# Threshold attention and a SwiGLU block on one core: another order for the first loads, and weight steps that begin one segment later

## The chip, the core and the metric

The kernel runs on one core of one Trainium2 chip. The metric is the device time of one execution in microseconds. The median of three runs of the kernel before is 1515.48 us (1515.47 to 1515.57).

## The reference

Attention over 8 batches of 8 heads, 576 positions, head width 64, with a threshold on the scores, then a gated block of width 512 to 1536 to 512 on the 4608 rows that come out:

```python
scores = scale * np.matmul(q, k.transpose(0, 1, 3, 2))
thresh = np.max(scores, axis=-1, keepdims=True) - tau
scores = np.where(scores >= thresh, scores, -1000000000.0)
scores = scores - np.max(scores, axis=-1, keepdims=True)
attn = np.exp(scores)
attn = attn / (np.sum(attn, axis=-1, keepdims=True) + 1e-09)
x = np.matmul(attn, v)          # heads side by side: (4608, 512)
g = x @ w_gate
out = (g / (1 + np.exp(-g)) * (x @ w_val)) @ w_out
```

Queries, keys and values arrive as 32-bit floats, the three weight matrices as 64-bit floats.

## The kernel before

**Work units.** Two heads of one batch make a pair; a batch has four pairs, and there are 32. A tile is 128 query rows of a pair (64 at the end of it). The main loop goes over segments, each with one pair and a list of its tiles. The first eight segments belong to batch 0: segments 0 to 3 take the first two tiles of pairs 0, 1, 2, 3; segments 4 to 7 take the remaining three tiles of pairs 3, 0, 1, 2. All later segments hold a whole pair. In this text the tiles are numbered as they come: T0 to T7 are the eight tiles of segments 0 to 3, and T8, T9, T10 those of segment 4.

**One tile.** `scores` multiplies queries by keys on PE (line 342 in part one; lines 342 and 347 in segments 4 to 7), DVE takes the maximum (L369), ACT makes the threshold (L375) and the exponential (L376), DVE drops what is under the threshold and sums (L380), then adds up and inverts the sums (L404, L405). In tiles T0 to T7 the inverse is put in a diagonal (L416) and enters with the transposition on PE (L448, L451); from T8 on, the rows are scaled before it, one head by ACT (L388) and the other by POOL (L386), and PE transposes them (L446). ACT copies the transposed rows out of PSUM (L454, L459), and one tile later PE multiplies by the values (`attend_tile`, L474 and L478) and ACT copies the product (L480). Scores have two PSUM tiles, so the next tile's L342 waits for L380 of the tile before.

**Preparing a pair.** Keys and queries come into SBUF in rows and are turned in 32x32 blocks on DVE. Queries are scaled first, by POOL (L254). `prepare` turns the keys (L815) and the first 256 query columns (L818); the remaining 320 columns of each query go on a list, `later`, and are turned when there is place for them, in `prepare` (L823) or in segment 4 (L893). The raw keys and queries of pairs 1 and 2 lie in a free buffer, `extra`; all other pairs share one pair of tiles of the pool `ld`, so that a new pair may be loaded only when the old one has been turned.

**Weights.** A weight piece is 768 KB of 64-bit floats. `fetch_weights` loads it (L185, two transfers of 384 KB) into one of a few places, and stops when none is free. `split_weights` makes a high word (L196) and a low word (L197) of it on ACT; there are two buffers for low words. `join_weights` puts them together, with three operations on DVE (L203, L207, L210) and one on POOL (L212), and sets the place free. A tile has at most one such step; `need(n)` makes more on the spot when the block's next product needs `n` pieces and fewer are joined. T10 has a double step.

**The order of the work.** Every engine takes its instructions in the order in which the program writes them. SP issues the loads. From segment 4 on, `fill` puts products of the second block (L536, `pg` and `pv`) between the parts of each tile; `pace` sets how many. `gates` multiplies the gate on POOL (L568). ACT's Exp table is loaded once at the start (L263).

Of the kernel before, what the change touches and what calls it, by code (L numbers as in the profile page):

```python
# [13 lines left out]
AF = mybir.ActivationFunctionType  # L14
ALU = mybir.AluOpType
# [4 lines left out]
def kernel(  # L20
# [30 lines left out]
    nc = tc.nc  # L51
    P = 128
    B, H, S, D = q.shape
    NP = H // 2
# [3 lines left out]
    G = 32  # L58
    NG = P // G
    NJ = S // G  # L60
# [7 lines left out]
    XB = 5  # L68
# [5 lines left out]
    QA = TA * P  # L74
    SCALE = 1.0 / float(D) ** 0.5
# [16 lines left out]
    tau_s = const.tile([P, 1], F32, name="tau_s")  # L92
    cut = const.tile([P, 1], F32, name="cut")
    cap = const.tile([P, 1], F32, name="cap")
    scl = const.tile([P, 1], F32, name="scl")
# [4 lines left out]
    minus2 = const.tile([P, 1], F32, name="minus2")  # L100
    nc.vector.memset(minus2, -2.0)
    junk = const.tile([P, 1], F32, name="junk")
# [6 lines left out]
    free = NP * (S - TA * P)  # L109
# [20 lines left out]
    XW, HW = NCC * TC, NF2 * P  # L130
    xall = const.tile([P, XB * XW + 2 * HW], F32, name="xall")
# [4 lines left out]
    extra = const.tile([P, 3 * NF2 * DM2], F32, name="extra")  # L136
# [36 lines left out]
    def fetch_weights(n=1):  # L173
        for _ in range(n):
            if not wpieces or wpieces[0][2] in used:
                return
            dst, srcs, place = wpieces.popleft()
            used.add(place)
            m = 2 if len(srcs) == 2 else nf
            to = places[place].bitcast(U64).rearrange("p (m n) -> p m n", m=m)  # L180
            if len(srcs) == 1:
                nc.sync.dma_start(out=to, in_=srcs[0])
            else:
                for x, src in enumerate(srcs):
                    nc.sync.dma_start(out=to[:, x, :], in_=src)  # L185
            fetched.append((dst, place))
# [44 lines left out]
    def load_qk(i):  # L231
        b, hp_ = divmod(i, NP)
        tiles = {}

        free = {1: 0, 2: 1}.get(i)
        srcs = {"q": (q, "(j r) (e d) -> e r j d"),
                "k": (k, "(j r) (e d) -> e r j d" if b == 0 else "(r j) (e d) -> e r j d")}
        for x, name in enumerate("qk"):
            if free is None:
                tiles[name] = ld.tile([P, NJ, G], F32, name=f"{name}raw")  # L240
            else:
                n = 2 * free + x
                tiles[name] = extra[:, n * S:(n + 1) * S].rearrange("p (j d) -> p j d", d=G)
        raws = [tiles[name].rearrange("p j d -> p (j d)") for name in "qk"]

        def load(name, js, queues):
            src, order = srcs[name]
            for g in range(NG):
                h, e = divmod(g, 2)
                queues[g // 2].dma_start(out=tiles[name][g * G:(g + 1) * G, js],  # L250
                                         in_=src[b, 2 * hp_ + h].rearrange(order, r=G, d=G)[e][:, js])

        def scale(cs):
            nc.gpsimd.tensor_scalar(out=raws[0][:, cs], in0=raws[0][:, cs], scalar1=scl, scalar2=None, op0=ALU.mult)  # L254

        if i == 0:

            both = [nc.sync, nc.scalar]
            load("k", slice(0, NJ), both)
            nc.scalar.dma_start(out=tau_s, in_=tau.partition_broadcast(P))  # L260
            load("q", slice(0, QA // G), both)

            nc.scalar.activation(junk, minus2, AF.Exp)  # L263
            nc.vector.tensor_scalar(out=scl, in0=tau_s, scalar1=0.0, scalar2=SCALE, op0=ALU.is_ge, op1=ALU.mult)
            nc.vector.tensor_scalar(out=cap, in0=tau_s, scalar1=0.0, scalar2=2e38, op0=ALU.is_ge, op1=ALU.mult)
            nc.vector.tensor_scalar(out=cap, in0=cap, scalar1=-1e38, scalar2=None, op0=ALU.add)
            nc.vector.scalar_tensor_tensor(out=cut, in0=tau_s, scalar=-1.0, in1=cap, op0=ALU.mult, op1=ALU.min)

            def load_rest():
                load("q", slice(QA // G, NJ), [nc.sync] * 2)  # L270
                scale(slice(QA, S))

            more_loads.append(load_rest)
        else:
            for name in "kq" if i == 1 else "qk":
                load(name, slice(0, NJ), [nc.sync] * 2)
            scale(slice(0, S))
            while more_loads:
                more_loads.pop()()
        return raws  # L280

    def load_v(seg):
# [481 lines left out]
    segs = [{"i": i, "tiles": early, "halved": False} for i in range(NP)]  # L764
# [27 lines left out]
        return rate  # L792

    raws = {}
    more_loads = []
    kept = {}
    later = []

    def fetch_qk(i):
        if i < NPAIR and i not in raws and i not in kept:  # L800
            raws[i] = load_qk(i)

    def prepare(seg):

        i = seg["i"]
        if i in kept:
            seg.update(kept[i])
            return
        qr, kr = raws[i]
        kept[i] = None  # L810
        qT = qkp.tile([P, S], F32, name="qT")
        if i < NP:
            kT = pall[:, 4 + i, :]
            rest = flat[:, i * (S - QA):(i + 1) * (S - QA)]
            nc.vector.transpose(out=kT, in_=kr)  # L815
            if i == 0:
                nc.vector.tensor_scalar(out=qr[:, 0:QA], in0=qr[:, 0:QA], scalar1=scl, scalar2=None, op0=ALU.mult)
            nc.vector.transpose(out=qT[:, 0:QA], in_=qr[:, 0:QA])  # L818

            later.append((rest, qr[:, QA:S]))  # L820
            if i >= NP - 2:
                to, fr = later.pop(0 if i == NP - 2 else -1)
                nc.vector.transpose(out=to, in_=fr)  # L823
            kept[i] = {"kT": kT, "qT": rest, "q0": QA}
        else:
            kT = qkp.tile([P, S], F32, name="kT")
            nc.vector.transpose(out=kT, in_=kr)
            nc.vector.transpose(out=qT, in_=qr)
        seg.update(kT=kT, qT=qT, q0=0)

    def give(n):
        for u in segs[n]["gives"]:
            ready.append(u)
            left[0] += cost(u)
        gains[n] = (gains[n][0], 0)
# [2 lines left out]
    fetch_qk(0)  # L838
    prepare(segs[0])
    fetch_qk(1)  # L840
    fetch_weights(2)
    load_v(segs[0])
    fetch_weights(2)
    prev, last = None, iter(())
    for n, seg in enumerate(segs):
        if NP <= n < 2 * NP:
            seg["v"] = segs[seg["i"]]["v"]
        for x, t in enumerate(seg["tiles"]):
            go = scores(seg, t)
            next(go)  # L850
            if not n and not x:
                run_idle(6)
            next(last, None)
            attends = prev is not None and x == 1
            products = iter(())
            attend_tile()
            next(go)
            next(last, None)
            flip()
            if n == NP and x == 0:  # L860
                attend_tile()
                give(n - 1)
            if n == 2 * NP and x == 1:
                give(n - 1)
            if attends and n > 2 * NP:
                if prev["i"] % NP == 0:
                    need(NW)
                    start_batch(prev["i"] // NP)
                products = attend(prev)
            part = pace(n, x) / 2  # L870
            more = len(split)
            if n or x:
                split_weights()
                fetch_weights(2)
            if x == 0 and n >= NP:
                fetch_qk(seg["i"] + 1)
            next(go)
            double = t == NT and NP <= n < NP + 2
            if more and not double:
                join_weights()  # L880
            fill(part)
            next(go)
            fill(part)
            if double:

                join_weights(2)
                split_weights()
                fetch_weights(2)
            gates()
            last = go  # L890
            if n == NP and later:
                to, fr = later.pop(0)
                nc.vector.transpose(out=to, in_=fr)  # L893
            if attends and n > 2 * NP:
                next(products)
                next(products)
                give(n - 1)
            if attends and seg["halved"]:
                load_v(seg)
            if x == 0 and 0 < n < NP:  # L900
                load_v(seg)
            if x == len(seg["tiles"]) - 2 and n + 1 < len(segs):
                prepare(segs[n + 1])
                if n < NP:
                    fetch_qk(segs[n + 1]["i"] + 1)
        prev = seg
    next(last)
    next(last)
# [40 lines left out]
```

## Time and profile before

| | us | share |
|---|---|---|
| span | 1513.8 | |
| PE busy | 1486.9 | 98% |
| DVE busy | 995.8 | 66% |
| ACT busy | 726.2 | 48% |
| POOL busy | 641.2 | 42% |
| first weight product (L536) begins | 66.97 | |

The shares are means over the span. In the first 67 us PE only does attention, and its work waits on chains through DVE and ACT; later the weight products fill it. The tables that the prediction shows come from three views: busy time by stretches (with the granted PE clock, 1.00 being full speed), instructions in order of time (start, length, engine, line, operands, and in brackets the idle time before it and what ended it), and the issues of transfers in the same list, under the names SPq and ACTq.

### The profile page before, as it was taken

To read this page: it belongs to the slowest core of one execution; us is meant where nothing else is said; L and a number is where in the kernel's file an instruction comes from. 1 tells how busy PE (TensorE), PEld (TensorE's weight loads), DVE (VectorE), ACT (ScalarE), POOL (GpSimd) and SP (SyncE) were. 2 spreads that over 40 slices of the span, in tenths; PEclk is the share of its full clock that TensorE was granted. 3 is DMA by queue.
4 is the path that set the end of the run, shared out by engine and by line. 5 is a ranking of instruction groups with operands and counts; after the bars stand their busy time and mean duration, and the time that the engine had idled before them with its cause. 6 is when DMAs were issued, how large, how long until landed. Compare 5 with 4: busy or idle time off the path is not lost. (4 is left out here: it accounts for less than half of the span.)

```text
span 1513.8 us, 31488 instructions
## 1 busy us (share of the span) xinstructions
PE 1486.9 (98%) x11808; PEld 1126.7 (74%) x11808; DVE 995.8 (66%) x3040; ACT 726.2 (48%) x2158; POOL 641.2 (42%) x637
## 2 busy tenths in 40 slices
PE   8999899999999999999999999999999999999999
PEld 6777664477777777787777777777777777888887
DVE  6878988777777777747767666776676767512212
ACT  5877665555455555434545444454544454311110
POOL 2355544367453545336444444553545353500000
PEclk9999999999999999999999999999999999999999
DMA  8542411211112111112111111211110220000000
GB/s 184 156 140 92 100 37 39 54 33 32 47 32 47 31 23 35 40 31 41 38 21 33 25 47 33 46 33 47 33 33 15 47 48 16 1 14 1 15 15 15
DMA packets 176872, 66.93 MB, mean 44 GB/s; under 512 B 159696, under 2 KB 159696, under 8 KB 176720
## 3 DMA queue, kind: packets, MB, share of 16 engines
q1 hardware_dynamic: 172416, 56.83, 16.5%
q0 software_dynamic: 2432, 7.87, 1.4%
q8 instruction: 94, 1.54, 0.4%
q14 instruction: 58, 0.48, 0.1%
q10 hardware_dynamic: 1872, 0.21, 0.1%
HBM read 55.44 MB, written 9.44 MB: 43 GB/s over the span
## 5 line engine op out<-in xcount | busy, mean ns | idle before, releaser
L386 POOL TENSOR_SCALAR pall<-pall,ri 128x288 f32<-128x288 f32 (+1 forms) x260 | 265.2, 1030 | 344.7 <-DVE ri L396 314.2
L536 PE MATMUL pv<-xall,wgv 128*128 128x256 f32 x1728 | 405.6, 383 | 3.0 <-ACT pall L454 2.7
L536 PE MATMUL pg<-xall,wgv 128*128 128x256 f32 x1728 | 403.2, 382 | 0.2 <-ACT pall L454 0.2
L536 PEld LDWEIGHTS pv<-xall,wgv 128*128 128x128 f32 x1728 | 324.7, 191 | 68.8 <-issue 21.9
L536 PEld LDWEIGHTS pg<-xall,wgv 128*128 128x128 f32 x1728 | 323.6, 190 | 65.5 <-issue 22.0
L357 DVE TENSOR_REDUCE mx<-sc 128x2 f32<-128x576 f32 x252 | 180.5, 750 | 237.4 <-PE sc L334 236.6
L380 DVE SCALAR_TENSOR_TENSOR pall<-sc,th,pall 128x288 f32<-128x288 f32 (+1 forms) x540 | 258.0, 527 | 33.2 <-ACT pall L376 33.2
L376 ACT ACTIVATE pall<-sc,nm 128x288 f32<-128x288 f32 (+1 forms) x540 | 236.3, 510 | 0.6
L372 ACT ACTIVATE th<-nm,cut 128x4 f32<-128x4 f32 (+1 forms) x140 | 41.6, 297 | 383.7 <-DVE nm L361 383.7
L568 POOL TENSOR_TENSOR ht<-ht,gt 128x512 f32<-128x512 f32 x84 | 107.0, 1274 | 194.1 <-DVE ht L556 105.8
L425 DVE STREAM_TRANSPOSE pall<-pall 128x576 f32<-128x576 f32 x252 | 181.3, 754 | 2.8 <-POOL pall L386 2.8
L634 PE MATMUL po<-wo,ht 128*128 128x256 f32 x768 | 177.5, 381 | 0.0
L334 PE MATMUL sc<-kT,qT 64*32 64x288 f32 x4032 | 157.9, 410 | 11.2 <-DVE pall L380 9.9
L634 PEld LDWEIGHTS po<-wo,ht 128*128 128x128 f32 x768 | 144.6, 190 | 26.4 <-issue 6.0
L556 DVE SCALAR_TENSOR_TENSOR ht<-tn,pv 128x512 f32<-128x512 f32 x102 | 69.9, 685 | 132.0 <-PE pv L536 118.7
L388 ACT ACTIVATE pall<-pall,ri 128x288 f32<-128x288 f32 (+1 forms) x264 | 132.9, 553 | 0.0
L310 ACT COPY sums<-sums 32x4 f32<-32x4 f32 (+1 forms) x560 | 108.4, 194 | 49.9 <-DVE pall L380 38.6
L549 ACT ACTIVATE tn<-pg 128x512 f32<-128x512 f32 x108 | 64.8, 600 | 139.8 <-PE pg L536 133.0
L500 PE MATMUL xa<-pall,vall 64*64 64x288 f32 x2016 | 128.7, 405 | 0.0
L334 PEld LDWEIGHTS sc<-kT,qT 64*32 64x32 f32 x4032 | 58.7, 105 | 88.8 <-issue 60.0
L500 PEld LDWEIGHTS xa<-pall,vall 64*64 64x64 f32 x2016 | 74.4, 133 | 50.7 <-ACT sums L310 3.6
L652 POOL TENSOR_TENSOR ht<-ht,xall 128x256 f32<-128x256 f32 x48 | 34.1, 727 | 156.3 <-PE po L634 155.1
(106 smaller groups left out, 1339.5 us busy)
## 6 DMA issues: line engine op xcount, KB each, us to landing
vall<-in_v_dram SPq DMA_DIRECT2D x112, 144.0 KB, 3.5
kraw<-in_k_dram SPq DMA_DIRECT2D x118, 72.0 KB, 2.9
qraw<-in_q_dram SPq DMA_DIRECT2D x116, 72.0 KB, 2.5
out_dram<-ob POOLq DMA_DIRECT2D x28, 256.0 KB, 2.9
wo<-in_moe_w_gate_dram SPq DMA_DIRECT2D x16, 384.0 KB, 3.7
wo<-in_moe_w_val_dram SPq DMA_DIRECT2D x16, 384.0 KB, 4.3
xall<-in_moe_w_out_dram SPq DMA_DIRECT2D x5, 768.0 KB, 4.9
wo<-in_moe_w_out_dram SPq DMA_DIRECT2D x3, 768.0 KB, 4.6
```

The source lines that it names most:

```text
L310: nc.scalar.copy(out, in_[:, :, 0])
L334: nc.tensor.matmul(ps[g * G:(g + 1) * G, h, 0:SH], qT[hs, col + a * G:col + (a + 1) * G], kT[hs, c * SH:(c + 1) * SH], start=True, stop=True)
L357: nc.vector.tensor_reduce(out=mx[:, 2 * x:2 * x + 2, 0], in_=tile_[:, :, 0:SH], axis=AX.X, op=ALU.max, negate=True)
L376: nc.scalar.activation(ps[x], scs[x], AF.Exp, bias=nm[:, x:x + 1])
L380: nc.vector.scalar_tensor_tensor(out=ps[x], in0=scs[x], scalar=th[:, x:x + 1], in1=ps[x], op0=ALU.is_ge, op1=ALU.mult, accum_out=sm[:, x, ...
L386: nc.gpsimd.tensor_scalar(out=ps[x], in0=ps[x], scalar1=ri[:, x:x + 1], scalar2=None, op0=ALU.mult)
L388: nc.scalar.activation(ps[x], ps[x], AF.Copy, scale=ri[:, x:x + 1])
L425: nc.vector.transpose(out=p, in_=p)
L500: nc.tensor.matmul(xa[a][h * D:(h + 1) * D, at:at + n * G].rearrange("d (i q) -> d i q", q=G), vr[rs, h, j, :], p[rs, lo:lo + n, j, :], st ...
L536: nc.tensor.matmul(ps[:, i], wgv[:, mat, c, (f + i) * P:(f + i + 1) * P], x[:, c, cs], start=(c == 0), stop=(c == NCC - 1))
L568: eng.tensor_tensor(out=hts[x], in0=hts[x], in1=gt, op=ALU.mult)
L634: nc.tensor.matmul(ps, h(f), w[:, f, :], start=(f == 0), stop=(f == NF2 - 1))
```

## The change

At the start, the change loads only what the first eight tiles use: keys and the first 256 query columns, of all four pairs. Pairs 0 and 1 use the queues of SP and ACT, the values of pair 0 follow, then pair 2, two weight pieces, pair 3, and two more pieces. The remaining query columns come in segments 1 to 3, pair 3's first. Pair 3 gets a place of its own in `xall`, so that only pair 0 lies in the shared tiles of `ld` in batch 0. Three remaining parts, instead of two, are turned in segment 4. Pair 4 is loaded in segment 4 instead of segment 3. Weight steps begin with the third tile instead of the second. Its aim is that the first pairs aren't held up by weights and by query columns that are used only later.

```diff
-        free = {1: 0, 2: 1}.get(i)
+        places_ = {1: extra[:, 0:2 * S], 2: extra[:, 2 * S:4 * S], 3: xall[:, XB * XW:XB * XW + 2 * S]}
...
-        if i == 0:
-            both = [nc.sync, nc.scalar]
-            load("k", slice(0, NJ), both)
-            nc.scalar.dma_start(out=tau_s, in_=tau.partition_broadcast(P))
-            load("q", slice(0, QA // G), both)
-            nc.scalar.activation(junk, minus2, AF.Exp)
...
+        if i < NP:
+            queues = [nc.sync, nc.scalar if i < 2 else nc.sync]
+            load("k", slice(0, NJ), queues)
+            if i == 0:
+                nc.scalar.dma_start(out=tau_s, in_=tau.partition_broadcast(P))
+            load("q", slice(0, QA // G), queues)
...
+            else:
+                scale(slice(0, QA))
             def load_rest():
                 load("q", slice(QA // G, NJ), [nc.sync] * 2)
                 scale(slice(QA, S))
             more_loads.append(load_rest)
         else:
-            for name in "kq" if i == 1 else "qk":
+            for name in "qk":
                 load(name, slice(0, NJ), [nc.sync] * 2)
             scale(slice(0, S))
-            while more_loads:
-                more_loads.pop()()
...
-            if i >= NP - 2:
-                to, fr = later.pop(0 if i == NP - 2 else -1)
+            if i == NP - 1:
+                to, fr = later.pop()
                 nc.vector.transpose(out=to, in_=fr)
...
     fetch_qk(1)
+    nc.scalar.activation(junk, minus2, AF.Exp)
+    load_v(segs[0])
+    fetch_qk(2)
     fetch_weights(2)
-    load_v(segs[0])
+    fetch_qk(3)
     fetch_weights(2)
...
-            if n or x:
+            if 0 < n < NP and x == 0:
+                if n == 1:
+                    more_loads.rotate(1)
+                    more_loads.popleft()()
+                more_loads.popleft()()
+            if n:
                 split_weights()
                 fetch_weights(2)
...
                 prepare(segs[n + 1])
-                if n < NP:
-                    fetch_qk(segs[n + 1]["i"] + 1)
```

More of the change, by code (lines that the diff above doesn't have):

```diff
@@ L238, in load_qk @@
         for x, name in enumerate("qk"):
-            if free is None:
+            if i in places_:
+                tiles[name] = places_[i][:, x * S:(x + 1) * S].rearrange("p (j d) -> p j d", d=G)
+            else:
                 tiles[name] = ld.tile([P, NJ, G], F32, name=f"{name}raw")
-            else:
-                n = 2 * free + x
-                tiles[name] = extra[:, n * S:(n + 1) * S].rearrange("p (j d) -> p j d", d=G)
         raws = [tiles[name].rearrange("p j d -> p (j d)") for name in "qk"]
@@ L254, in scale @@
             nc.gpsimd.tensor_scalar(out=raws[0][:, cs], in0=raws[0][:, cs], scalar1=scl, scalar2=None, op0=ALU.mult)
-        if i == 0:
-            both = [nc.sync, nc.scalar]
-            load("k", slice(0, NJ), both)
-            nc.scalar.dma_start(out=tau_s, in_=tau.partition_broadcast(P))
-            load("q", slice(0, QA // G), both)
-            nc.scalar.activation(junk, minus2, AF.Exp)
[L264 to L267, printed above, removed]
+        if i < NP:
[4 more added lines that the diff above has]
+            load("q", slice(0, QA // G), queues)
+            if i == 0:
+                nc.vector.tensor_scalar(out=scl, in0=tau_s, scalar1=0.0, scalar2=SCALE, op0=ALU.is_ge, op1=ALU.mult)
+                nc.vector.tensor_scalar(out=cap, in0=tau_s, scalar1=0.0, scalar2=2e38, op0=ALU.is_ge, op1=ALU.mult)
+                nc.vector.tensor_scalar(out=cap, in0=cap, scalar1=-1e38, scalar2=None, op0=ALU.add)
+                nc.vector.scalar_tensor_tensor(out=cut, in0=tau_s, scalar=-1.0, in1=cap, op0=ALU.mult, op1=ALU.min)
+            else:
+                scale(slice(0, QA))
             def load_rest():
@@ L794 @@
     raws = {}
-    more_loads = []
+    more_loads = deque()
     kept = {}
```

## The prediction

> **What bounds the kernel now.** I read the page first (busy shares), then a table of stretches, then the engines' instructions in order of time for the first 100 us, then the DMA issues. The page says PE is busy for 98% of the span; the table of stretches says where it isn't (columns: PE, PEld, DVE, ACT, POOL busy, granted PE clock, DMA share, GB/s):
>
> ```profile
> 20.00:28.00 8.00, 8.00 (x68) 6.28 (x67) 4.02 (x10) 5.55 (x13) 2.07 (x2) 1.00 0.89 182
> 28.00:32.00 4.00, 0.27 (x2) 0.03 (x2) 3.67 (x8) 1.91 (x5) 1.42 (x1) 1.00 0.48 90
> ...
> 34.00:38.00 4.00, 4.00 (x26) 2.58 (x24) 2.85 (x4) 1.55 (x5) 3.50 (x2) 0.50 0.94 253
> ...
> 168.00:172.00 4.00, 1.24 (x33) 0.43 (x32) 3.93 (x14) 3.23 (x10) 2.33 (x3) 1.00 0.28 108
> 172.00:176.00 4.00, 4.00 (x24) 3.04 (x11) 3.82 (x12) 1.34 (x5) 2.38 (x2) 0.57 0.02 4
> ...
> 300.00:1500.00 1200.00, 1199.51 (x9530) 935.60 (x9523) 751.27 (x2382) 525.19 (x1652) 507.70 (x535) 1.00 0.14 30
> ```
>
> From 300 us on PE never rests. The change edits only the first 100 us and leaves PE's own instructions and their order as they are. So what PE loses or saves before 300 us goes into the end one for one. Two idle stretches cost twice, because after each the granted clock is 0.50.
>
> The first hole is a late load of pair 2's keys:
>
> ```profile
> 27.92 0.78 DVE L815 STREAM_TRANSPOSE pall<-extra 128x576 f32<-128x576 f32 x1 [2.86 <-DMA extra<-in_k_dram]
> ...
> 32.02 3.07 PE L342 MATMUL sc<-pall,qT 64*128 64x288 f32 x8 [3.75 <-DVE pall L380]
> ...
> 35.02 1.97 PE L474 MATMUL xa<-pall,vall 128*64 128x128 f32 x16
> ```
>
> I number the tiles T0 to T7 (part one) and T8, T9, T10 (the next segment). The time of a tile's first threshold multiply (L380) is my marker: T2 20.99, T3 31.05, T4 38.81, T5 45.93, T6 52.08, T7 57.82 us. In steady state one tile takes 5.74 us (52.08 to 57.82); T3 took 10.06 and T4 7.76.
>
> The second place to see is T8, at 66 to 75 us, where PE meets POOL's scaled probabilities:
>
> ```profile
> 65.75 1.87 POOL L386 TENSOR_SCALAR pall<-pall,ri 128x576 f32<-128x576 f32 x1 [1.91 <-DVE ri L405]
> ...
> 67.96 0.50 DVE L893 STREAM_TRANSPOSE pall<-extra 128x320 f32<-128x320 f32 x1
> ...
> 70.19 1.36 PE L342 MATMUL sc<-pall 64*128 64x288 f32 x10
> ...
> 71.48 1.09 PE L446 MATMUL tp<-pall 128*128 128x128 f32 x8
> ...
> 74.51 2.86 PE L536 MATMUL pv<-xall,wgv 128*128 128x256 f32 x12 [1.40 <-ACT pall L454]
> ```
>
> POOL's L386 ends at 67.62, long before PE's transposes (L446) want it at 72.0.
>
> **What the Trainium skill says.** "TensorE: Matmul & The Clock Gate", Part 1, gives two clock states, and half speed after an idle window of about 3.4 us. The trace agrees and is stricter: the 3.75 us hole was followed by half clock from 32.2 to 39.0 us, and the hole of 2.60 us at 168 by 3.4 us of it. "DMA: Bandwidth & Descriptors", Issuing engines are not separate DMA queues, says that a second issuing queue saves issue time only. I use this for the keys that move to ACT's queue; the trace shows about 0.5 us per issue (4 in 2.12 us at 6.11).
>
> **Part by part.**
>
> *Loads (keys and first queries at once, weights behind).* Pair 2's keys and first queries now stand before all weights: 24 transfers come before the last key transfer, none of them weights, against 40 with eight weight transfers. At 0.53 us per issue on SP, and with the two waits at 3 to 5 us that are there today, the keys are issued by about 11 us and the queries by 13.5; 2.5 us later they have landed. T2's transposes then follow its multiplies at 23.0 without the wait of 2.86 us, and without the weight join that stood before them (0.54+0.56+0.96 = 2.06 us on DVE). T3: transposes end at 24.1, maxima 24.1, exponentials 25.8, L380 at 26.6 instead of 31.05. That is -4.4 us. T0 to T2 stay: their chain runs over PE and ACT (xa L474, then its copy L480 at 19.86, then L375 at 20.02), and the ACT weight step removed in T1 (1.97 us) lay beside PE's work.
>
> *Values of pair 1.* T4 needs them. Now 53 transfers stand before them instead of 41; the 12 more are pair 3's keys, first and remaining queries, which the change issues first. Before, they were issued so:
>
> ```profile
> 25.89 0.50 SPq L296 DMA_DIRECT2D vall<-in_v_dram  x1
> ...
> 27.63 0.51 SPq L297 DMA_DIRECT2D vall<-in_v_dram  x1
> ```
>
> and landed 2.8 us later, at 30.4. In the built program each transfer waits for the one eight before it (the query at 17.74 is issued just when the value load of 12.24 has landed, 5.5 us after). I stepped the new order through with this rule, 0.5 us per issue, 0.54 us of DMA time per 72 KB of keys, 1.15 us per weight transfer, rates fitted to the transfers of before: pair 1's values land at 33.5 us, with 32 to 36 as ends. Without the wait T4's product (L474) would start at 29.7. PE so idles 3.8 us, the clock falls again, and T4's L474 with its tail L478 takes 2.6 us, as before (35.02 to 37.6). From there L480, L375 and L376 take 1.2 us: T4's L380 at 37.3 instead of 38.81. Net -1.5 us of the -4.4; ends -3 (32 us) and +1 (36 us). I take -1.3, a little off for a slower clock in T5. After that DVE sets T5 (join 2.06 and three transposes 1.4) in both kernels.
>
> *Pair 4's queries on POOL: the added wait.* Pair 0's remaining queries keep their place in the load buffer until T8, where L893 turns them. Before, they were turned at 28.95 (L823). Pair 4's queries use the same buffer, were loaded at 44.36, and are now loaded in T8. In the built program their transfers wait for exactly that L893, and POOL's scaling of them (L254) stands in POOL's queue *before* T8's L386. So L386, and behind it the weight joins' last adds (L212), wait for L893, four transfers and a scaling. The trace has this very chain once:
>
> ```profile
> 43.83 0.47 DVE L823 STREAM_TRANSPOSE pall<-qraw 128x320 f32<-128x320 f32 x1
> ...
> 44.36 1.95 SPq L250 DMA_DIRECT2D qraw<-in_q_dram  x4
> ...
> 48.88 1.73 POOL L254 TENSOR_SCALAR qraw<-qraw,scl 128x576 f32<-128x576 f32 x1 [4.03 <-DMA qraw<-in_q_dram]
> ```
>
> 4.58 us from L823's end (44.30) to the scaling, then 1.73. On T8's clock of before: L893 ends at 68.0 (L207 takes 0.56 instead of 0.98 beside an idle POOL), scaling 72.6 to 74.3, L386 to 76.2. PE has done the first head's transposes at 72.0 and waits 4.2 us; behind it stand the second head's four, then pg, then pv. pv starts at 77.4 instead of 74.51: +2.9 us, since it had idled 1.40 before. Ends +2 and +3.5.
>
> *Clock after that.* A hole of 4.2 us leaves some window mostly idle; 3.4 us at half clock cost up to 1.7 us of PE work, 6.8 us up to 3.4. I take +1.7, ends 0.8 and 3.4.
>
> *Weight steps from the third tile on.* One join less in part one: seven pieces are joined by T10 instead of eight, and the gate of the third and fourth blocks needs eight. The missing one comes as an extra step there: DVE 2.06, POOL 1.81, and ACT's split (L197) has only two buffers for its low words and waits for these adds, as it already does for 2.82 us at 88.15. Copy L480 stands behind that split and goes from 89.1 to 90.7; pv at 89.37 waits for its buffer: +1.6 us, ends 0.5 and 2.5. The matmul that needs the eighth piece comes only at 88.7, when the add (86.6) is done.
>
> *Nothing:* the third L893 (0.5 us, DVE idles 2.4 us at T11); splitting the scalings (POOL idles then); the Exp table load behind four more issues on ACT (done near 8, needed at 9.51).
>
> Sum: -1.3 + 2.9 + 1.7 + 1.6 = +4.9, so 1515.5 + 4.9 = 1520.4 us.
>
> **Rivals.**
> *A, they cancel:* values land near 30, no hole in T4. Then T4's L380 is at 32.2, -6.6 us, against +6.2: 1515.1. For it: key and query bytes ahead of the values grow by only 256 KB. Against: eight more issues on SP alone are 4 us.
> *B, faster:* as A, and PE bridges POOL's delay with work in hand: -6.6 + 1.6 = 1510.5. Against: PE takes its queue in order, and pg and pv stand behind the transposes.
> *C, clearly slower:* values land at 36 (+1), both clock losses at their upper end (3.4), queue +3.5, step +2.5: 1525.9.
>
> **How the numbers follow.** Forecast case 0.60, A 0.20, B 0.12, C 0.08. The bound of 0.2% is 3.0 us. Nearly all of the forecast case and C lie above it: slower 0.67; A and the forecast's low end: same 0.19; B and a little of A: faster 0.14. The range from 1512 to 1525 reaches past A on the low side and leaves out B and C, 2 in 10 together.
>
> **What would show it.** Right: no DMA wait before L815 in T2; a PE hole before T4's L474; POOL's L386 in T8 beginning some 9 us after its reciprocal instead of at once, with L254 ahead of it; a PE hole of about 4 us between the halves of T8's L446; 0.50 in the clock column after each. Wrong: T4's L474 at full clock near 30 us (A or B), or L446 in T8 without a hole (B).

## The result, and the profile after

The changed kernel takes 1523.6 us (median of 6 runs, 1523.1 to 1524.7), the kernel before 1515.4 in the same runs. The ratio is 1.0056, with a 95% interval of 1.0043 to 1.0069: 8 us slower, well clear of the noise. From here on line numbers are those of the changed kernel: behind `load_qk` most are one lower (L379 was L380, L385 was L386, L445 was L446, L479 was L480, L535 was L536), in it L249 was L250 and L253 was L254, and the turning of remaining queries in segment 4, L893, is now L902.

First the table of stretches of the changed kernel (columns as in the prediction):

```profile
28.00:32.00 4.00, 1.50 (x10) 0.88 (x8) 3.77 (x9) 3.01 (x6) 0.00 (x0) 1.00 0.85 162
34.00:38.00 4.00, 3.67 (x23) 2.63 (x24) 0.00 (x0) 0.52 (x3) 2.36 (x3) 0.50 0.61 108
72.00:80.00 8.00, 4.36 (x13) 3.73 (x14) 6.44 (x11) 4.99 (x10) 8.00 (x4) 0.66 0.54 133
92.00:96.00 4.00, 1.90 (x12) 1.25 (x10) 4.00 (x8) 1.76 (x2) 1.75 (x1) 1.00 0.58 171
...
300.00:1500.00 1200.00, 1198.71 (x9563) 931.40 (x9564) 755.24 (x2402) 530.40 (x1668) 509.12 (x535) 1.00 0.14 30
```

From 300 us on PE is full, as before. In 72 to 80 us PE now works 4.36 of 8 us at a clock of 0.66 while POOL works all 8, where the kernel before had

```profile
72.00:80.00 8.00, 6.61 (x51) 4.63 (x50) 6.42 (x13) 6.29 (x13) 3.69 (x2) 1.00 0.14 30
```

The stretch from 92 to 96 has a hole of its own. The first hole (28 to 32) is still there, with PE busy for 1.50 us instead of 0.27, but another transfer is late now, as the next lines show.

**Part one.** Instructions of the changed kernel in order of time, and below them the issues of two of the four transfers that bring pair 1's values:

```profile
23.00 0.78 DVE L814 STREAM_TRANSPOSE pall<-extra 128x576 f32<-128x576 f32 x1
...
26.50 0.82 DVE L379 SCALAR_TENSOR_TENSOR pall<-sc,th,pall 128x576 f32<-128x576 f32 x1 [1.09 <-ACT pall L375]
...
33.85 0.66 PE L473 MATMUL xa<-pall,vall 128*64 128x128 f32 x2 [4.36 <-DMA vall<-in_v_dram]
34.85 1.94 PE L473 MATMUL xa<-pall,vall 128*64 128x128 f32 x14 [0.34 <-DMA vall<-in_v_dram]
...
31.30 0.41 SPq L295 DMA_DIRECT2D vall<-in_v_dram  x1
...
32.95 0.51 SPq L296 DMA_DIRECT2D vall<-in_v_dram  x1
```

Pair 2's keys are turned at 23.00 without the wait of 2.86 us, and T3 is 4.5 us earlier (26.50 instead of 31.05). T4's product then waits 4.36 us for pair 1's values, whose transfers are issued 5.4 us later than before (31.30 instead of 25.89).

**T8.** The queue of POOL, and what PE does behind it:

```profile
64.80 0.17 DVE L404 RECIPROCAL ri<-tot 128x2 f32<-128x2 f32 x1
...
66.92 0.50 DVE L902 STREAM_TRANSPOSE pall<-qraw 128x320 f32<-128x320 f32 x1
...
67.46 1.95 SPq L249 DMA_DIRECT2D qraw<-in_q_dram  x4
...
71.86 1.72 POOL L253 TENSOR_SCALAR qraw<-qraw,scl 128x576 f32<-128x576 f32 x1 [8.63 <-DMA qraw<-in_q_dram]
73.56 2.03 POOL L385 TENSOR_SCALAR pall<-pall,ri 128x576 f32<-128x576 f32 x1
...
75.64 1.12 PE L445 MATMUL tp<-pall 128*128 128x128 f32 x4 [4.12 <-POOL pall L385]
...
77.62 4.59 PE L535 MATMUL pv<-xall,wgv 128*128 128x256 f32 x12
```

L385's input has been ready since 65 us (L404 ends at 64.97), but it stands behind L253, which waits for pair 4's queries, and these are issued at 67.46, just when L902 has ended. The twelve `pv` matmuls took 2.86 us before and take 4.59 at the lower clock.

**T10.** In this stretch the kernel before had

```profile
82.76 1.02 DVE L203 TENSOR_SCALAR wgv<-wgv 128x768 f32<-128x768 f32 x2
...
85.73 4.16 POOL L212 TENSOR_TENSOR wgv<-wgv,extra 128x768 uint32<-128x768 uint32 x2 [6.05 <-DVE wgv L210]
...
88.15 1.01 ACT L197 ACTIVATE extra<-wo,minus 128x768 f32<-128x768 uint32 x1 [2.82 <-POOL wgv L212]
...
89.37 1.99 PE L536 MATMUL pv<-xall,wgv 128*128 128x256 f32 x8 [0.31 <-ACT xall L480]
```

and the changed kernel has

```profile
89.67 2.64 DVE L203 TENSOR_SCALAR wgv<-wgv 128x768 f32<-128x768 f32 x2
...
89.89 1.99 POOL L212 TENSOR_TENSOR wgv<-wgv,extra 128x768 uint32<-128x768 uint32 x1 [8.05 <-DVE wgv L210]
94.25 4.16 POOL L212 TENSOR_TENSOR wgv<-wgv,extra 128x768 uint32<-128x768 uint32 x2 [2.37 <-DVE wgv L210]
...
96.67 0.99 ACT L197 ACTIVATE extra<-wo,minus 128x768 f32<-128x768 uint32 x1 [2.91 <-POOL wgv L212]
97.57 0.24 ACT L479 COPY xall<-xa 128x128 f32<-128x128 f32 x1
...
97.86 3.29 PE L535 MATMUL pv<-xall,wgv 128*128 128x256 f32 x8 [3.96 <-ACT xall L479]
```

The extra step's add (89.89) is the new one. The two clips (L203) of the double step take 2.64 us beside it instead of 1.02. PE's wait for the copy (L480 before, L479 after) grows from 0.31 to 3.96 us.

Put together on PE's instructions, where both kernels have the same ones:

| from, to | before, us | after, us | difference |
|---|---|---|---|
| start to the first weight product (L535) | 66.97 | 66.35 | -0.6 |
| to T8's `pv` | 7.54 | 11.27 | +3.7 |
| to T10's scores (L347; L346 after) | 2.79 | 4.52 | +1.7 |
| to T10's `pv` | 12.07 | 15.72 | +3.65 |
| to the next scores (L342; L341 after) | 1.92 | 3.22 | +1.3 |
| to the end of the span | 1422.5 | 1421.8 | -0.7 |

The sum is 9.1 us, the difference of the two spans (1522.9 and 1513.8). The profiled execution of the changed kernel was one of the two slowest of six, so this is 0.9 us more than the 8.2 of the medians.

### The profile page after: what moved, and what is told of

Its sections match the earlier page's. It is cut to its first block, busy times and chain, and to the rows that moved or that the text cites. A ratio compares the mean times of both kernels' runs of the same rounds, so it can differ in the third digit from the quotient of the medians.

```text
span 1522.9 us, 31512 instructions
## 1 busy us (share of the span) xinstructions
PE 1489.3 (98%) x11808; PEld 1128.7 (74%) x11808; DVE 997.8 (66%) x3040; ACT 727.6 (48%) x2158; POOL 643.9 (42%) x640
## 5 line engine op out<-in xcount | busy, mean ns | idle before, releaser
L535 PE MATMUL pv<-xall,wgv 128*128 128x256 f32 x1728 | 408.1, 385 | 5.2 <-ACT xall L479 4.0
L385 POOL TENSOR_SCALAR pall<-pall,ri 128x288 f32<-128x288 f32 (+1 forms) x260 | 266.4, 1035 | 337.8 <-DVE ri L395 317.1
L535 PE MATMUL pg<-xall,wgv 128*128 128x256 f32 x1728 | 403.5, 382 | 0.0
L535 PEld LDWEIGHTS pv<-xall,wgv 128*128 128x128 f32 x1728 | 326.7, 192 | 71.9 <-issue 22.3
L535 PEld LDWEIGHTS pg<-xall,wgv 128*128 128x128 f32 x1728 | 323.8, 190 | 64.9 <-issue 22.0
L379 DVE SCALAR_TENSOR_TENSOR pall<-sc,th,pall 128x288 f32<-128x288 f32 (+1 forms) x540 | 258.1, 528 | 38.2 <-ACT pall L375 38.2
L633 PEld LDWEIGHTS po<-wo,ht 128*128 128x128 f32 x768 | 144.6, 190 | 26.5 <-issue 6.0
```

The lines of the kernel that those rows point to most:

```text
L379: nc.vector.scalar_tensor_tensor(out=ps[x], in0=scs[x], scalar=th[:, x:x + 1], in1=ps[x], op0=ALU.is_ge, op1=ALU.mult, accum_out=sm[:, x, ...
L385: nc.gpsimd.tensor_scalar(out=ps[x], in0=ps[x], scalar1=ri[:, x:x + 1], scalar2=None, op0=ALU.mult)
L535: nc.tensor.matmul(ps[:, i], wgv[:, mat, c, (f + i) * P:(f + i + 1) * P], x[:, c, cs], start=(c == 0), stop=(c == NCC - 1))
L633: nc.tensor.matmul(ps, h(f), w[:, f, :], start=(f == 0), stop=(f == NF2 - 1))
```

## The experiments

Three theories had to be told apart. One: T8's queue and T10's extra step are two separate losses. Two: they are one loss, and the second only follows the first. Three: the late values in part one cost most, and the rest is small. All kernels start from the changed one. Each ratio is to the kernel before, in the same runs.

**Pair 0's rest turned early.** Its remaining queries are turned in `prepare`, together with pair 3's, and no longer in T8, so that their buffer is free for pair 4.

```diff
             if i == NP - 1:
-                to, fr = later.pop()
-                nc.vector.transpose(out=to, in_=fr)
+                for at in (-1, 0):
+                    to, fr = later[at]
+                    del later[at]
+                    nc.vector.transpose(out=to, in_=fr)
```

> The changed kernel, but pair 0's remaining queries are turned beside pair 3's in T4 instead of in T8, so that pair 4's queries can be loaded before T8. My theory (POOL's queue makes the hole in T8): L385 of T8 starts at most 4 us later than its reciprocal instead of 9, the hole of 4.12 us between the halves of L445 and the half clock after it are gone (-3.7 and -1.7 us), the loss in T10 stays: 1518.2 us. Rival (PE would wait at T8 or T9 anyway, for DVE or ACT; the hole only shows where): 1522 us or more.

Measured: 1520.3 us, ratio 1.0035 [1.0021, 1.0048]; 3.3 us of the 8 are back, where 5.4 were expected. PE, in order of time:

```profile
72.80 0.66 PE L445 MATMUL tp<-pall 128*128 128x128 f32 x4 [0.47 <-POOL pall L385]
...
93.20 2.07 PE L535 MATMUL pv<-xall,wgv 128*128 128x256 f32 x4 [3.95 <-ACT xall L479]
```

T8's wait falls from 4.12 to 0.47 us, and from the first weight product to `pv` it takes 7.5 us, as in the kernel before; from there to T10's scores 2.8 us, as before too. So T8 gives back the whole 5.4 us in this profile. Part one is 0.8 us longer in it (first weight product at 67.16), and what else the median lost these traces do not show. T10's wait stays at 3.95. So T10's loss does not come from T8's.

**Weight steps from the second tile on.**

```diff
-            if n:
+            if n or x:
                 split_weights()
                 fetch_weights(2)
```

> The changed kernel, with weight steps from the second tile on, as before. My theory (the step that is missing at T10 costs 3.65 us of PE's wait for L479 and 1.3 us of half clock there): no extra step in T10, pv there waits under 1 us, about 1519 us, with up to 1 us given back in T1 because the first weight piece lands at 17.9. Rival (T10 is late because T8 was late, not for the extra step): 1523 us, the wait in T10 stays near 4 us.

Measured: 1519.4 us, ratio 1.0027 [1.0016, 1.0038]. The mirror image:

```profile
75.11 0.88 PE L445 MATMUL tp<-pall 128*128 128x128 f32 x4 [3.59 <-POOL pall L385]
...
92.58 0.70 PE L535 MATMUL pv<-xall,wgv 128*128 128x256 f32 x2 [0.31 <-ACT xall L479]
```

T10's wait falls to 0.31 us, T8's stays (3.59 us).

**Both.** If the losses are separate, the gains add up.

> The changed kernel with pair 0's remaining queries turned early and the weight steps from the second tile on, and the values left where they are. If T8's and T10's holes are what made the change slower and stand in different stretches, their two gains add up (3.3 and 4.2 us alone): 1516.1 us, level with the kernel before. If they share a cause (one hole hides the other), the gain is that of the larger alone, 1519 to 1520.

Measured: 1516.3 us, ratio 1.0009 [1.0000, 1.0017]. They add up. The two edits take back 7.3 of the 8.2 us, and the changed order of the loads is then worth about nothing, although T3 starts early in it. Its T3 comes at 28.78 (31.05 before), but its first weight product only at 67.82 (66.97 before), and T4 again waits for pair 1's values. So the question was where T3's gain went.

**Pair 1's values before pair 3.**

```diff
     fetch_qk(2)
     fetch_weights(2)
+    load_v(segs[1])
     fetch_qk(3)
...
-            if x == 0 and 0 < n < NP:
+            if x == 0 and 1 < n < NP:
                 load_v(seg)
```

> The changed kernel, with pair 1's values loaded behind the first two weight pieces and ahead of pair 3's keys. My theory (T4's hole of 4.36 us is only the wait for these values): T4's L473 starts near 29.7 at full clock, T4's L379 at 32.2 instead of 38.60, 1517.2 us. Rival (the transfers only change places, and pair 3's keys or the next weight pieces now come late): L379 of T5 at 44 or later instead of 45.73, 1522 us.

Measured: 1520.5 us, ratio 1.0033 [1.0021, 1.0046]. T4 has its values and its marker comes at 32.25 us, as expected. The first weight product starts at 62.7 instead of 66.35. The late values were a third loss, then, but only about half of what was expected came back (3.1 of 6.4 us), for T5's marker comes 8.5 us after T4's (40.76; the rival had said 44 or later), with a new hole. POOL, ACT and PE of this kernel:

```profile
33.12 1.08 POOL L253 TENSOR_SCALAR xall<-xall,scl 128x320 f32<-128x320 f32 x1 [5.54 <-DMA xall<-in_q_dram]
34.18 1.61 POOL L253 TENSOR_SCALAR qraw<-qraw,scl 128x320 f32<-128x320 f32 x1
35.76 2.38 POOL L212 TENSOR_TENSOR wgv<-wgv,extra 128x768 uint32<-128x768 uint32 x1
...
38.18 0.98 ACT L197 ACTIVATE extra<-wo,minus 128x768 f32<-128x768 uint32 x1 [3.08 <-POOL wgv L212]
...
39.51 2.03 PE L447 MATMUL tp<-pall 128*128 128x128 f32 x8 [2.88 <-ACT pall L415]
```

The scalings of the remaining queries (L253) head POOL's queue and wait for their transfers. The first weight add (L212) was due at 30.6, when its VectorE part (L210) was done. ACT's third L197 needs the low-word buffer that this add frees, and L415, the next thing PE needs, stands behind L197. It is T8's mechanism again, in part one, which in the changed kernel was hidden behind the wait for the values.

**All three edits.**

> All three edits together. My theory: the three losses are separate and add up, -5.4 -4.9 -6.4 from 1523.6: 1507 us, 0.5% under the kernel before. Rival (part one is bound by DVE and ACT, and what is won there is lost to a weight piece that lands late for the second tile, or to later waits): 1512 to 1515 us.

Measured: 1517.7 us, ratio 1.0019 [1.0012, 1.0027], nearly 11 us above what was expected, and above the rival's range too. T8's and T10's holes are gone, and the one in part one has grown, because with steps from the second tile on the adds are due earlier (25.8):

```profile
33.42 1.08 POOL L253 TENSOR_SCALAR xall<-xall,scl 128x320 f32<-128x320 f32 x1 [6.52 <-DMA xall<-in_q_dram]
...
35.53 3.57 POOL L212 TENSOR_TENSOR wgv<-wgv,extra 128x768 uint32<-128x768 uint32 x2
...
37.36 0.99 ACT L197 ACTIVATE extra<-wo,minus 128x768 f32<-128x768 uint32 x1 [6.20 <-POOL wgv L212]
```

The expectation had failed, and the queue on POOL was only a reading of the trace. So it was taken away.

**The scaling queued late.** The load stays where it is. Its scaling goes into POOL's queue at the end of the second tile of the segment, behind that tile's weight add.

```diff
             def load_rest():
                 load("q", slice(QA // G, NJ), [nc.sync] * 2)
-                scale(slice(QA, S))
+                unscaled.append(lambda: scale(slice(QA, S)))
...
             last = go
+            while x == 1 and unscaled:
+                unscaled.popleft()()
```

> The kernel with all three edits, and one more: the scaling of a remaining query load is queued on POOL at the end of the second tile of its segment, behind that tile's weight add, and no longer with the load. If POOL's queue was what ate the three edits' sum (scalings that wait for late queries stand ahead of the weight adds, ACT waits for the adds' low-word buffers), the hole before T4 goes, T4's marker comes at 32.3 us instead of 39.9, L197 in T3 runs without its 6.2 us of idle time, the FFN starts at about 60.5 and the kernel takes about 1509 us (60.5 plus the 1448.7 us that the kernel with three edits took from there on). If instead the transfers as such were late (the weights and the values now queue ahead of each other), T4 still waits, for a DMA, at 36 us or later, and the time stays at 1514 to 1518 us.

Measured: 1512.5 us, ratio 0.9984 [0.9977, 0.9991]: clearly faster than the changed kernel, and 0.16% faster than the kernel before. POOL, then ACT:

```profile
32.80 1.81 POOL L212 TENSOR_TENSOR wgv<-wgv,extra 128x768 uint32<-128x768 uint32 x1 [4.30 <-DVE wgv L210]
34.59 1.09 POOL L253 TENSOR_SCALAR xall<-xall,scl 128x320 f32<-128x320 f32 x1
...
31.16 1.08 ACT L197 ACTIVATE extra<-wo,minus 128x768 f32<-128x768 uint32 x1
```

L197 has no idle time before it where it had 6.20 us, T4's marker comes at 34.3 instead of 39.9, and the first weight product starts at 63.7 instead of 69.0. That is 5 us of the nearly 9 that were expected, and the time lies between the two theories. The trace decides for the first: no product of T4 waits for a transfer. The expectation took T4's 32.3 from a kernel that begins its weight steps with the third tile. Here T3 comes 2.1 us later than there (28.6 against 26.5): 0.9 us of it stood from the first tile on in this profile, and the step in the second tile stands before pair 2's transposes on VectorE. Another 1.2 us is lost between T4 and the first weight product, where the granted clock was 0.76 from 43 to 50 us.

**The same with steps from the third tile on.**

> As the one before, but with the weight steps from the third tile on again, as in the changed kernel. If the extra step in T10 costs what the trace of the changed kernel showed (a hole 3.65 us longer than need be and some clock after it), this is 3.5 to 5 us slower than the one before, about 1513.5 us. If the step fewer in the second tile helps the first part (no weight work on DVE and ACT while the first tiles are due) as much as it costs in T10, the two are equal.

Measured: 1515.8 us, ratio 1.0002 [0.9994, 1.0010], 3.3 us slower than with the step. Part one does reach T4 at 32.1 and the first weight product at 60.4, as the expectation before had it. T10 then loses it again: a hole of 3.95 us (82.5 to 86.4), and 6.8 us at half clock. At the scores behind T10 this profile is 2.1 us behind that of the kernel with the step, where at the first weight product it was 3.4 us ahead. The profiled execution took 1513.97 us, 1.8 us less than the median, so it shows where the loss arises and not its whole size.

**The late scaling alone, on the changed kernel.**

> The changed kernel with only the late scaling. In it T4 waits for pair 1's values, and POOL's late adds are hidden behind that: the T4 hole stays (33.7 us and on), T8's and T10's holes stay, and the time is within 1 us of the changed kernel's 1523.6. If POOL's queue were what holds T4 in the changed kernel, T4 would come 3 us or more earlier and the time would fall to 1520 or below.

Measured: 1524.6 us, ratio 1.0062 [1.0048, 1.0075], the changed kernel's time. T4's marker comes at 39.2. POOL's queue in part one is no cause of this result; it only stands in the way of the cure.

**Double steps, one after the other.** For T10's size: the extra step is there, but a double step now does all four operations for its first piece, then for its second.

```diff
         for up, place, lo in steps:
             nc.vector.tensor_scalar(out=up, in0=up, scalar1=1.875 * 2.0 ** -80, scalar2=2.0 ** -111,
                                     op0=ALU.min, op1=ALU.max)
-        for up, place, lo in steps:
             ub = up.bitcast(U32)
             nc.vector.tensor_scalar(out=ub, in0=ub, scalar1=3, scalar2=None, op0=ALU.logical_shift_left)
-        for up, place, lo in steps:
-            ub = up.bitcast(U32)
             nc.vector.scalar_tensor_tensor(out=ub, in0=words(place, up, 1), scalar=0x80000000, in1=ub,
```

> The kernel with late scaling and steps from the third tile on, with one more edit: two weight steps joined together go step by step (clip, shift, combine, add for the first, then the same for the second) and no longer operation by operation. In T10 of the kernel without the edit, VectorE's two clips take 2.64 us beside POOL's add of the step before, and the first of the double step's adds starts only at 82.83 and ends at about 85.1, which ScalarE's L197 and behind it L479 wait for. If the size of T10's hole is set by how late that first add starts, it now starts at about 81.3, L197 starts 1.8 us earlier (83.4), the hole on TensorE shrinks from 3.9 to about 2.1 us, and the stretch at half clock behind it (6.8 us) may go: 1511.5 to 1514 us, against 1515.8. If instead the number of steps (three in one tile) sets it, whatever their order, L197 starts within 0.4 us of 85.25 and the time stays at 1515.8.

Measured: 1513.95 us, ratio 0.9990 [0.9982, 0.9998], against 1.0002 [0.9994, 1.0010] without the edit (two sets of runs, each beside the kernel before; the intervals overlap a little, from 0.9994 to 0.9998). The trace is the better witness (L206 here is the shift, L207 the combining operation, L209 the add). VectorE, POOL, ACT:

```profile
78.23 0.55 DVE L203 TENSOR_SCALAR wgv<-wgv 128x768 f32<-128x768 f32 x1
78.82 2.05 DVE L206 TENSOR_SCALAR wgv<-wgv 128x768 uint32<-128x768 uint32 x1
...
78.46 2.00 POOL L209 TENSOR_TENSOR wgv<-wgv,extra 128x768 uint32<-128x768 uint32 x1 [5.38 <-DVE wgv L207]
82.01 1.98 POOL L209 TENSOR_TENSOR wgv<-wgv,extra 128x768 uint32<-128x768 uint32 x1 [1.55 <-DVE wgv L207]
...
84.03 1.00 ACT L197 ACTIVATE extra<-wo,minus 128x768 f32<-128x768 uint32 x1 [1.70 <-POOL wgv L209]
```

L197 starts 1.2 us earlier than at 85.25 (1.8 expected), and PE's hole is 2.8 us instead of 3.95. So the order of the steps and not their number alone sets the size of the hole. The miss of 0.6 us is in the second line: VectorE's shift (to 80.87) lasts until just after POOL's add has ended, at 80.46. The half clock did not go: it again lasted 6.8 us. Of the 1.9 us between the two medians the traces show only these 1.2 us; the two profiled spans themselves are nearly equal (1512.5 and 1512.2).

**The same edit where T10 has two steps.**

> The same edit on the kernel with late scaling and steps from the second tile on. There T10 has two steps and no hole of note (L535 waits 0.31 us for L479), so by the same theory there is at most that 0.3 us, and 0.9 us of DVE order, to win: 1511.5 to 1512.8 us, against 1512.5.

Measured: 1511.8 us, ratio 0.9976 [0.9966, 0.9985], within the expectation, and not to be told from the 0.9984 without the edit.

## Why it went as predicted, and where the terms were off

The direction and the mechanisms held: early keys in T2, the wait for the values in T4, POOL's queue in T8, ACT's low-word buffer in T10, and half clock after the holes. The forecast of 1520.4 was 3.2 us too low. On the two spans it is 4.2 (9.1 instead of 4.9), and the terms tell where.

*Part one, -1.3 predicted, -0.6 measured.* T3 came at 26.50 (26.6 predicted), the first values at 33.9 (33.5). What followed was slower: the values arrived in two portions, so that L473 and L477 lasted from 33.85 to 37.41, 3.6 instead of 2.6 us, and T4 came at 38.6 instead of 37.3.

*POOL's queue in T8, +2.9 predicted, +3.7 measured.* The wait was right (4.2 predicted, 4.12 measured). The other 0.8 us is clock: the half speed began at 74.5 (0.75 was granted from 74 to 75 us, 0.50 from 75 to 81), so already the second four L445 took 1.12 us instead of 0.66. Turning pair 0's queries early took this term and the next away.

*Clock after that, +1.7 predicted, +1.7 measured* on `pv` alone; with the 0.8 us above, the clock cost 2.5 us in T8. That the figures for `pv` agree is in part luck: in the kernel with the late scaling alone, which waits 3.51 us at the same place, the same twelve `pv` took 3.21 us and not 4.59.

*The extra step in T10, +1.6 predicted, +3.65 measured, and 1.3 of clock behind it that the prediction had not counted.* This is the most mis-sized term. The prediction counted 2.06 us of VectorE work and let 1.6 of it reach the copy; here the 2.06 us enter in full (87.61 to 89.67). The rest is the double step's two L203, which run beside the extra step's add on POOL and take 1.62 us more than before. 2.06 + 1.62 = 3.68 us, by which the double step's adds, and L197 behind them, came later. The prediction left this out, although in T8 it had read a shift as slower beside POOL (0.98 us instead of 0.56).

The Trainium skill, "SBUF — State Buffer", Who interferes with whom, says that VectorE in a two-port mode and GpSimd (POOL here) contend for a shared port pair: the one that issues first has it for the whole instruction, and the other "fully blocks". The traces agree in part. The second L203, 0.54 us alone, took 2.11 us and ended 0.4 us after POOL's add; with the operations in another order it was the shift that did so (2.05 us instead of 0.56). But the shift that started 0.3 us after POOL's L386 in T8 of the kernel before took only 0.98 us and ended at 67.05, before L386 did (67.62). In which mode these operations work no run shows, and that the port is the cause was not measured apart.

Together: of the 4.2 us, the wait in T10 makes 2.05, the clock 2.1 (0.8 and 1.3) and part one 0.7; from the scores behind T10 to the end of the span the changed kernel is 0.7 us shorter, which nothing here explains.

The rivals A and B fell with T4's wait of 4.36 us (they had the values near 30 us and no hole there). C's late values (36 us) did not come. But its clock term of 3.4 us was nearer to the 3.8 us measured in T8 and T10 than the 1.7 of the forecast case, and the 8.2 us of the medians lie between the two, nearer to C (10.4) than to the forecast (4.9).

## What to carry to other kernels

An instruction that waits for a transfer is better queued not when the transfer is issued, but behind the work that its engine can do meanwhile: here, moving the scalings of the remaining queries on POOL was worth 5 us (1517.7 to 1512.5), and only showed once the wait that hid it had gone. When weight work is moved from a slack tile into a full one, count it on every engine there, and look in the trace for how long its operations take beside the other engine's, not just alone: here two clips took 2.64 instead of 1.02 us beside an add on POOL. And a stage that starts earlier is worth only as much as the next late input allows: list the arrival of every input of the next tile before pricing the gain.

## What the runs showed that was not expected

A clip on VectorE that takes 0.54 us alone took 2.11 us, and a shift that takes 0.56 us took 2.05, when they started 0.3 to 0.4 us after an add on POOL, and the combining operation (L210) took 2.44 instead of 0.96 us in T8 beside POOL's L212.

In single executions, the length of a hole didn't settle the stretch at half clock behind it. Three kernels of this study had a hole of 1.3 us before 43 us, with PE busy for 3.68 of the 5 us from 38 to 43 in each. From 43 to 50 us PE was granted 0.76 with the late scaling, 1.00 with that and steps from the third tile on, and 0.51 with the late scaling, steps from the second tile on and step-by-step joins:

```profile
43.00:50.00 7.00, 7.00 (x44) 5.40 (x45) 5.75 (x12) 5.55 (x13) 2.88 (x2) 0.76 0.76 211
```

```profile
43.00:50.00 7.00, 7.00 (x68) 5.28 (x64) 6.53 (x13) 6.67 (x16) 3.15 (x3) 1.00 0.57 158
```

```profile
43.00:50.00 7.00, 7.00 (x36) 4.76 (x34) 4.76 (x9) 4.62 (x10) 2.86 (x2) 0.51 0.74 186
```

What decides between them stays open. Each line is from one execution, and the 17 executions of the first of these kernels spread over 3.5 us (1510.9 to 1514.4), as much as such a stretch can cost (7 us at 0.51 do 3.4 us less work). So the stretch may differ between executions of one and the same kernel as well, which no run here shows.
